# mLSTM and mixture of experts on one core: heads paired in another way, and the third expert's weights loaded at seven set places

## The chip, the cores and the metric

The kernel runs on 1 core of one Trainium2 chip. The metric is the device time in microseconds (us), the median of several executions. A core has TensorE (PE in the profile; its weight loads are PEld), VectorE (DVE), ScalarE (ACT), GpSimd (POOL) and SyncE (SP), which here issues most of the DMAs.

## The reference

First an mLSTM over 4 batches, 8 heads, 768 time steps and a head width of 40; then a mixture of 8 experts, to which each of the 3072 tokens goes by its largest logit.

```python
for t in range(S):
    m_new = np.maximum(f_gate[:, :, t] + m, i_gate[:, :, t])
    f_stab = np.exp(f_gate[:, :, t] + m - m_new)
    i_stab = np.exp(i_gate[:, :, t] - m_new)
    C = f_stab[:, :, None, None] * C + i_stab[:, :, None, None] * np.einsum('bhd,bhe->bhde', vt, kt)
    n = f_stab[:, :, None] * n + i_stab[:, :, None] * kt
    h_tilde = np.einsum('bhde,bhe->bhd', C, qt)
    denom = np.maximum(np.abs(np.einsum('bhd,bhd->bh', n, qt)[:, :, None]), 1.0)
    y[:, :, t] = 1.0 / (1.0 + np.exp(-o_gate[:, :, t])) * h_tilde / denom
...
expert_idx = np.argmax(xn @ en.T / tau, axis=1)
for e in range(E):
    h = np.maximum(x[mask] @ w1[e], 0.0)
    out[mask] = gate_w[mask, None] * (h @ w2[e])
```

## The kernel before

**The mLSTM part** runs in 24 steps `n`; a step takes 128 time steps of one batch, as two chunks `c` of 64, with all 8 heads as four pairs `a` of two heads `r`. The order of every engine's work is the order in which the code is written. A step on TensorE is, in this order: `stage_add(n, 0)` adds the first chunk's keys times values to the state sums in PSUM (two products with `j40`, line 667, carry the old state `c_st` over; line 677 adds); `stage_scores(n + 1)` makes the next step's scores (line 640); every second step transposes (`px`) and logits (`pm`); `stage_y(n)` multiplies the weighed scores `w_s` by `uv` (line 715) and the queries `q_s` by the state (line 725; `c_st` for the first chunk, `c_mid` for the second); `stage_add(n, 1)` adds the second chunk to the sums (line 677 again; not in the last four steps). ACT copies the sums to `c_mid`, DVE to `c_st`; `uv` is made by POOL (line 626), which also multiplies by the output gate (line 762) and, in six of the steps 11 to 19, makes a piece of the first expert's weights (line 208).

Of a pair, one head lies in partitions 0 to 39 and the other in 64 to 103 of `q_s` and of the state; `uv` and the state are block diagonal, 2 x 41 columns wide, the second head's block to the right. In `stage_add` each pair is two products of 41 columns with the same weights, one to the upper and one to the lower half of the output's partitions. All these matmuls are fp32, and one product stands in the trace as two matmuls and two weight loads.

**The expert part.** The first two experts run early, on their first half of tokens and then on the second. The latter loop, in the program `mm1(exps[e]["ws"], xp, ...)` with 2 x 8 feature blocks `f`, makes the tiles `hh_b` (ACT, line 396) and `hl_b` (DVE, line 398) from `ph` (TensorE, line 394, 8 matmuls each, three buffers). Between the blocks, `do(3 - e)` takes small steps from the list `todo`: the order of the remaining experts (`order`), their token lists, the gather of the third expert's tokens (`tokens`, four indirect DMAs on POOL), then the 7 loads of the third expert's weights. Load 0 and 1 are 512 KB each, load 2 is 256 KB twice (to both halves), loads 3 to 6 are 320 KB each. SP first reads six expert numbers into registers (line 1572), then issues the loads. The buffers `raw` (7) are free by then. The pieces are cast by ACT (line 205) and completed by DVE (line 208) in the loop behind, `mm2` of `po_b`. Later experts' loads are issued as their buffers come free.

Of the kernel before, what the change touches and what calls it, by code (L numbers as in the profile page):

```python
# [22 lines left out]
B, H, S, D = 4, 8, 768, 40  # L23
# [3 lines left out]
P = 128  # L27
L = 64
NW = S // P
NP = H // 2  # L30
NS = NW * B
NC = S // L
FC = F // P
# [3 lines left out]
D1 = D + 1  # L37
# [11 lines left out]

W1_AT = (11, 13, 14, 16, 17, 19)  # L50
W_AT = (10, 12, 13, 15, 16, 18, 19, 20, 22, 22, 22, 23, 23)
XW = 3 * P
PAD = NT
MID = NT // 2
# [11 lines left out]
def tile_mlstm_moe(  # L66
# [22 lines left out]
    V, G, A, T, SY = nc.vector, nc.gpsimd, nc.scalar, nc.tensor, nc.sync  # L89
# [72 lines left out]
    def load_expert(e, at=None):  # L162
        raws, ws = {}, {}
        w1_, w2_ = (w[e] if at is None else w[ds(at, 1)].rearrange("o p f -> (o p) f") for w in (w1, w2))

        def load(i):
            def go():
                raw = raws[i] = wp.tile([P, F], F32, name=f"raw_{e}_{i}", tag="raw", bufs=7)
                if i < 2:
                    SY.dma_start(raw, w1_[i * P : (i + 1) * P])  # L170
                elif i == 2:
                    SY.dma_start(raw[0:L], w1_[2 * P : DM])
                    SY.dma_start(raw[L:P], w1_[2 * P : DM])
                else:
                    c = slice(2 * (i - 3), 2 * (i - 3) + 2)
                    SY.dma_start(
                        raw[:, 0 : 2 * DM].rearrange("p (c d) -> p c d", c=2),
                        w2_.rearrange("(c p) d -> p c d", p=P)[:, c],
                    )

            return go

        def load_half(i, half):
            def go():
                c = slice(half * 512, half * 512 + 512)
                if half == 0:
                    raws[i] = wp.tile([P, F], F32, name=f"raw_{e}_{i}", tag="raw", bufs=7)
                if i < 2:
                    SY.dma_start(raws[i][:, c], w1_[i * P : (i + 1) * P, c])
                else:  # L190
                    for r0 in (0, L):
                        SY.dma_start(raws[i][r0 : r0 + L, c], w1_[2 * P : DM, c])

            return go

        def piece(i, half, eng=None, on_act=True):
            def go():
                if i < 3:
                    c = slice(half * 512, half * 512 + 512)
                    h, lo, src = ws["w1h"][:, i, c], ws["w1l"][:, i, c], raws[i][:, c]  # L200
                else:
                    c = 2 * (i - 3) + half
                    h, lo, src = ws["w2h"][:, c], ws["w2l"][:, c], raws[i][:, half * DM : (half + 1) * DM]
                if on_act:
                    A.copy(h, src)  # L205
                else:
                    V.tensor_copy(h, src)
                (eng or V).tensor_tensor(lo, src, h.bitcast(F32), ALU.subtract)  # L208

            return go  # L210

        def tiles(pool, k):
            for t in "hl":
                shape = [P, 3, F] if k == 1 else [P, FC, DM]
                ws[f"w{k}{t}"] = pool.tile(shape, F32R, name=f"w{k}{t}_{e}", tag=f"w{k}{t}")

        return dict(ws=ws, tiles=tiles, load=load, load_half=load_half, piece=piece)


# [322 lines left out]
    with ExitStack() as actx:  # L542
# [22 lines left out]
        NH, NG, NB = B * H, NJ * B * H, 3  # L565
# [11 lines left out]
        k_e, k_o, q_s, kv_s, kr_s, vr_s, uv, w_s = [], [], [], [], [], [], [], []  # L577
# [55 lines left out]
        def stage_scores(n):  # L633
            q, k = divmod(n, 2)
            s = st.setdefault(n, {})["s"] = pS.tile([P, 2, NP, L], F32, name=f"s_{n}", tag="ps")
            for c in range(2):
                for a in range(NP):
                    for r, kk in ((0, k_e), (1, k_o)):
                        cs = slice(c * L, c * L + L)
                        T.matmul(  # L640
                            s[r * L : r * L + L, c, a],
                            kk[q % NB][:, k, a, cs],
                            q_s[q % NB][:, k, a, cs],
                            start=True,
                            stop=True,
                        )
# [12 lines left out]
        def stage_add(n, c):  # L659

            q, k = divmod(n, 2)
            if c == 0:
                st[n]["y"] = pY.tile([P, 512], F32, name=f"y_{n}", tag="py")
            pc = pcv(n)
            if c == 0 and n >= B:
                for r in range(2):
                    T.matmul(  # L667
                        pc[r * L : r * L + D],
                        j40,
                        c_st[n % B][:, :, r * D1 : (r + 1) * D1],  # L670
                        start=True,
                        stop=False,
                        skip_group_check=True,
                    )
            for a in range(NP):
                for r in range(2):
                    T.matmul(  # L677
                        pc[r * L : r * L + D, a],
                        kr_s[q % NB][:, k, c, a],
                        uv[n % NB][:, c, a, r],  # L680
                        start=n < B and c == 0 and a == 0,
                        stop=True,
                        skip_group_check=True,
                    )

        def state_rows(n, dst):
            for r in range(2):
# [20 lines left out]
        def stage_y(n):  # L708

            q, k = divmod(n, 2)  # L710
            y = st[n]["y"]
            for a in range(NP):
                ya = [y[c * L : c * L + L, a * 2 * D1 : (a + 1) * 2 * D1] for c in range(2)]
                for c in range(2):
                    T.matmul(  # L715
                        ya[c],
                        w_s[n % NB][:, c, a],
                        uv[n % NB][:, c, a].rearrange("p r d -> p (r d)"),
                        start=False,
                        stop=n < B and c == 0,  # L720
                        skip_group_check=True,
                    )
                for c, state in ((0, c_st[n % B]), (1, c_mid[n % 2])):
                    if n >= B or c:
                        T.matmul(  # L725
                            ya[c],
                            q_s[q % NB][:, k, a, c * L : c * L + L],
                            state[:, a],
                            start=False,
                            stop=True,  # L730
                            skip_group_check=True,
                        )
# [393 lines left out]
        def halves(t, n, r):  # L1126
            return t.rearrange("p (g r a) -> p g r a", r=2, a=NP)[:, :, r]
# [7 lines left out]
        for c in range(2):  # L1135
            for r in range(2):
# [4 lines left out]
                    start=True,  # L1141
                    stop=True,
                )
        for r in range(2):
            r0 = r * L
# [23 lines left out]
        gr = ap1.tile([NG, NK, NG], F32, name="gr")  # L1169
# [45 lines left out]
        def gates_turn():  # L1215
            n = NJ * B
            w = n * NP
            pt = pM.tile([P, 512], F32, name="pg1", tag="pm")
            for k in range(NK):
                for c in range(2):  # L1220
                    for r in range(2):
                        at_ = (k * 2 + c) * w
# [10 lines left out]
            for k in range(NK):  # L1233
                for r in range(2):
                    at_ = 8 * w + k * w
                    T.matmul(
                        pt[r * L : r * L + L, at_ : at_ + w].rearrange("p (g a) -> p g a", a=NP),
                        onef[0:NG, 0:L],
                        halves(gr[:, k], NG, r),
                        start=True,  # L1240
                        stop=True,
                    )
# [204 lines left out]
        def do(k):  # L1447
            for _ in range(k):
                if todo:
                    todo.pop(0)()  # L1450
# [118 lines left out]
    def where():  # L1569

        at.extend(
            nc.values_load(order[0:1, j : j + 1], engines=[ET.SP], min_val=0, max_val=E - 1) for j in range(NO)
        )
        exps[2] = load_expert(2, at[0])
        todo[:] += [exps[2]["load"](i) for i in range(7)]

    def tokens():
        nonlocal xs
# [5 lines left out]
    for e in range(NE):  # L1584
        for f in range(FC):
            mm1(exps[e]["ws"], xp, slice(e * HALF, (e + 1) * HALF), f, hs, slice(e * HALF, (e + 1) * HALF))
            do(3 - e)
            if f % 4 == 1:
                first_out(2 * e + f // 4, *first_outs[2 * e + f // 4])
        if e == 0:  # L1590
            exps[2]["tiles"](wp, 1)
            todo += beyond
# [202 lines left out]
def _layout(q, k, v, i_gate, f_gate, o_gate, moe_expert_emb, moe_tau, moe_w1, moe_w2):  # L1795
# [6 lines left out]

    def dims_first(a):

        a = a.reshape(B, NP, 2, NW, P, D).transpose(3, 0, 2, 5, 1, 4).reshape(NS // 2, 2, 2, D, NP, P)
        return c(a.transpose(0, 2, 3, 1, 4, 5))

    def both_heads(a):
# [50 lines left out]
```

## Time and profile before

| | |
|---|---|
| device time, median of 3 | 339.04 us (338.65 to 343.72) |
| the profiled execution | 340.7 us, its span 338.9 us |
| TensorE busy | 313.4 us, 92% of the span |
| VectorE busy | 219.3 us, 65% |
| ScalarE busy | 162.4 us, 48% |
| GpSimd busy | 146.1 us, 43% |
| TensorE's mean granted clock | 0.978 |
| HBM read and written | 172 GB/s over the span |

The span runs from the first to the last instruction; the profiled execution has 1.8 us around it. Of TensorE, busy time counts the whole modelled duration of each matmul, and consecutive ones overlap, so how dense it is shows better in the starts of its instructions than in this share. The mLSTM part ends at about 118 us, the early experts' part at about 193 us, and six experts follow.

### The profile page before, as it was taken

The page shows a single profiled execution, that of the slowest core. Times are in us where ns is not written, and L with a number is a line of the kernel's source. Part 1 is how long each engine was busy: PE and PEld are TensorE (multiplying, and loading weights), DVE is VectorE, ACT ScalarE, POOL GpSimd, SP SyncE. Part 2 cuts the span into 40 slices and gives each one's busy share as a digit, 9 for nine tenths or more (in the row PEclk, how much of TensorE's full clock was granted, in tenths as well). Part 3 has the DMA queues.
Part 4 walks back from the last instruction along what each step waited for, and adds up shares of the span by engine and source line. Part 5 has one row for each costly group of instructions (what it writes and reads, how often), then busy time and mean ns, then how long its engine had stood idle before and what let it go on. Part 6 is the DMA issues. An engine that isn't in the chain of part 4 may idle for free.

```text
span 338.9 us, 10523 instructions
## 1 busy us (share of the span) xinstructions
PE 313.4 (92%) x4120; PEld 296.4 (87%) x4121; DVE 219.3 (65%) x626; ACT 162.4 (48%) x429; POOL 146.1 (43%) x182
## 2 busy tenths in 40 slices
PE   8897989998988888999979999999999999999991
PEld 4786979887977778999969989999999999999991
DVE  6674677896885449996645595566566585685520
ACT  4655555566655484343325465254454463463410
POOL 6657757668787169040631711240250241322121
PEclk9997999999999799999979999999999999999997
DMA  7998687997998605020392887346447458431001
GB/s 228 289 307 258 200 267 240 288 296 250 309 319 240 236 21 155 2 77 3 112 306 94 232 238 222 118 125 190 122 127 224 126 151 223 119 91 39 12 10 45
DMA packets 29344, 58.57 MB, mean 173 GB/s; under 512 B 3851, under 2 KB 18392, under 8 KB 29286
## 3 DMA queue, kind: packets, MB, share of 16 engines
q1 hardware_dynamic: 26406, 48.91, 47.3%
q0 software_dynamic: 2624, 8.48, 8.4%
q8 instruction: 34, 0.56, 0.7%
q10 hardware_dynamic: 256, 0.43, 0.4%
q14 instruction: 24, 0.20, 0.2%
HBM read 49.98 MB, written 8.19 MB: 172 GB/s over the span
## 4 chain that ended last, share of the span: by engine, by line
PE 80%; issue 5%; DVE 4%; ACT 3%; DMA 3%; POOL 2%; another core or an unknown queue 1%; POOLq 0%; SPq 0%; DVEq 0%; ACTq 0%
PE ph L394 27%; PE po L432 17%; PE s L640 5%; PE y L715 4%; PE po_b L432 4%; PE po_a L432 3%; PE y L677 3%; PE y L725 3%; PE po L419 3%; PE pt L357 2%; PE warm L1078 2%; DMA kv_s<-in_rows 2%; PE px L792 2%; PE pm L812 1%; PE y L667 1%
## 5 line engine op out<-in xcount | busy, mean ns | idle before, releaser
L451 POOL DMA_INDIRECT out<-ob,ids x20 | 20.3, 1014 | 99.6 <-DVE ob L448 73.8
L626 POOL TENSOR_TENSOR uv<-kv_s,u_t 64x328 f32<-64x328 f32 x47 | 35.5, 754 | 17.5 <-PE y L677 11.2
L432 PE MATMUL po<-w2h,hh 128*128 128x320 f32 x128 | 40.3, 315 | 0.0
L432 PE MATMUL po<-w2l,hh 128*128 128x320 f32 x128 | 39.6, 309 | 0.0
L432 PE MATMUL po<-w2h,hl 128*128 128x320 f32 x128 | 39.6, 309 | 0.0
L396 ACT ACTIVATE hh<-ph 128x448 fp32r<-128x448 f32 (+2 forms) x48 | 23.6, 491 | 33.1 <-PE ph L394 31.4
L398 DVE SCALAR_TENSOR_TENSOR hl<-ph,hh 128x384 fp32r<-128x384 f32 (+1 forms) x48 | 24.5, 511 | 14.6 <-ACT hh L396 11.1
L715 PE MATMUL y<-uv,w_s 128*64 128x82 f32 x384 | 30.3, 246 | 3.2 <-issue 2.1
L640 PE MATMUL s<-q_s,k_o 128*64 128x64 f32 x384 | 28.2, 224 | 5.2 <-issue 5.1
L394 PE MATMUL ph<-xh,w1h 128*128 128x448 f32 (+2 forms) x96 | 32.2, 338 | 0.0
L394 PE MATMUL ph<-xh,w1l 128*128 128x448 f32 (+2 forms) x96 | 32.1, 337 | 0.0
L640 PEld LDWEIGHTS s<-q_s,k_o 128*64 128x64 f32 x384 | 24.9, 138 | 6.1 <-issue 6.1
L640 PE MATMUL s<-q_s,k_e 128*64 128x64 f32 x384 | 28.3, 224 | 1.0 <-DVE w_s L649 0.7
L725 PE MATMUL y<-c_mid,q_s 128*64 128x82 f32 x192 | 28.9, 240 | 0.0
L205 ACT CAST w1h<-raw 128x512 fp32r<-128x512 f32 x48 | 28.8, 616 | 0.0
L448 DVE TENSOR_SCALAR ob<-po,gts 128x320 f32<-128x320 f32 x16 | 8.8, 551 | 28.1 <-PE po L432 28.1
L715 PEld LDWEIGHTS y<-uv,w_s 128*64 128x64 f32 x384 | 21.9, 141 | 5.5 <-issue 3.6
L208 DVE TENSOR_TENSOR w2l<-raw,w2h 128x320 fp32r<-128x320 f32 x58 | 26.5, 494 | 0.2
L640 PEld LDWEIGHTS s<-q_s,k_e 128*64 128x64 f32 x384 | 24.8, 138 | 2.1 <-DVE w_s L649 0.8
L649 DVE TENSOR_TENSOR w_s<-s,late 128x512 f32<-128x512 f32 x24 | 16.5, 686 | 14.3 <-PE s L640 9.6
L205 ACT CAST w2h<-raw 128x320 fp32r<-128x320 f32 x62 | 25.2, 461 | 0.0
L693 ACT COPY c_mid<-y 40x164 f32<-40x164 f32 x48 | 14.0, 292 | 22.1 <-PE y L677 15.4
(327 smaller groups left out, 984.4 us busy)
## 6 DMA issues: line engine op xcount, KB each, us to landing
raw<-in_w SPq DMA_DIRECT2D x32, 320.0 KB
kv_s<-in_rows SPq DMA_DIRECT2D x23, 324.0 KB
raw<-in_w SPq DMA_DIRECT2D x14, 512.0 KB
q_s<-in_qt SPq DMA_DIRECT2D x11, 512.0 KB
raw<-in_w SPq DMA_DIRECT2D x18, 256.0 KB
sig<-in_og SPq DMA_DIRECT2D x24, 160.0 KB
x_d<-x SPq DMA_DIRECT2D x24, 160.0 KB
k_e<-in_kt SPq DMA_DIRECT2D x11, 160.0 KB
```

The source lines that it names most:

```text
L205: A.copy(h, src)
L208: (eng or V).tensor_tensor(lo, src, h.bitcast(F32), ALU.subtract)
L394: T.matmul(ph, lt, rh, start=i == 0, stop=i == len(ops) - 1)
L396: A.activation(hh, ph, AF.Relu)
L398: V.scalar_tensor_tensor(hl[:, 0:full], ph[:, 0:full], 0.0, hh[:, 0:full].bitcast(F32), ALU.max, ALU.subtract)
L432: T.matmul(po[0 : ts_.stop - ts_.start, 0:DM], lt[f][:, ts_], rh[:, f], start=k == 0, stop=k == len(ops) - 1)
L451: store = G.indirect_dma_start(out=out, out_offset=bass.IndirectOffsetOnAxis(ap=slots, axis=0), in_=ob, in_offset=None, bounds_check=NT - ...
L626: (eng[r] if eng else G).tensor_tensor(uv[n % NB][rows, :, :, r], vr_s[q % NB][rows, k], u_t[rows, j, b].unsqueeze(3).broadcast_to([L, 2, ...
L640: T.matmul(s[r * L : r * L + L, c, a], kk[q % NB][:, k, a, cs], q_s[q % NB][:, k, a, cs], start=True, stop=True,)
L649: V.tensor_tensor(w_s[n % NB].rearrange("p c a t -> p (c a) t"), st[n]["s"].rearrange("p c a t -> p (c a) t"), late.unsqueeze(1).broadcast ...
L715: T.matmul(ya[c], w_s[n % NB][:, c, a], uv[n % NB][:, c, a].rearrange("p r d -> p (r d)"), start=False, stop=n < B and c == 0, skip_group_ ...
L725: T.matmul(ya[c], q_s[q % NB][:, k, a, c * L : c * L + L], state[:, a], start=False, stop=True, skip_group_check=True,)
```

## The change

**First part.** The two heads of a pair `a` now stand side by side in the columns of the state sums, in the upper half of the partitions for even `a` and in the lower half for odd `a`. So `stage_add` makes one product of 82 columns for each pair (4 in place of 8 of 41 columns), and the state's column block `m` holds one head of each of two pairs. The keys, the queries and the decay factors are laid out accordingly by the host and by one set of matmuls at the start; `stage_scores` takes other blocks in the same number; in `stage_y` all eight products of line 715 come first, then those of line 725, which now write two runs of 41 columns.

**Second part.** The third expert's loads leave the list. Load `i` is issued after feature block `W2_AT[i]` of the 16, and VectorE writes one element of its buffer first, on which the DMA waits.

```diff
+W2_AT = (4, 6, 8, 10, 11, 13, 14)
...
-        def load(i):
+        def load(i, after=None):
             def go():
                 raw = raws[i] = wp.tile([P, F], F32, name=f"raw_{e}_{i}", tag="raw", bufs=7)
+                if after:
+                    after.memset(raw[0:1, 0:1], 0.0)
...
                 for a in range(NP):
-                    for r, kk in ((0, k_e), (1, k_o)):
-                        cs = slice(c * L, c * L + L)
+                    for r in range(2):
+                        m = a // 2 * 2 + r
                         T.matmul(
                             s[r * L : r * L + L, c, a],
-                            kk[q % NB][:, k, a, cs],
-                            q_s[q % NB][:, k, a, cs],
+                            (k_e, k_o)[a % 2][q % NB][:, k, m, cs],
+                            q_s[q % NB][:, k, m, cs],
...
             for a in range(NP):
-                for r in range(2):
-                    T.matmul(
-                        pc[r * L : r * L + D, a],
-                        kr_s[q % NB][:, k, c, a],
-                        uv[n % NB][:, c, a, r],
-                        start=n < B and c == 0 and a == 0,
+                r0, m = a % 2 * L, a // 2 * 2
+                T.matmul(
+                    pc[r0 : r0 + D, m : m + 2],
+                    kr_s[q % NB][:, k, c, a],
+                    uv[n % NB][:, c, a],
+                    start=n < B and c == 0 and a < 2,
...
+            for m in range(NP):
                 for c, state in ((0, c_st[n % B]), (1, c_mid[n % 2])):
                     if n >= B or c:
                         T.matmul(
-                            ya[c],
-                            q_s[q % NB][:, k, a, c * L : c * L + L],
-                            state[:, a],
+                            yp[c * L : c * L + L, m // 2, :, m % 2],
+                            q_s[q % NB][:, k, m, c * L : c * L + L],
+                            state[:, m].rearrange("p (q d) -> p q d", q=2),
...
         exps[2] = load_expert(2, at[0])
-        todo[:] += [exps[2]["load"](i) for i in range(7)]
...
             do(3 - e)
+            if e * FC + f in W2_AT:
+                exps[2]["load"](W2_AT.index(e * FC + f), V)()
```

On TensorE, from the end of `stage_y` of step 7 to the first scores of step 9, the rows before are these (a row is a product, with its line, output, inputs and columns; the number behind a name is a buffer's):

```order
L715 MATMUL y_928<-uv_154,w_s_155 64x82 x2
L725 MATMUL y_928<-c_st_165,q_s_146 64x82
L725 MATMUL y_928<-c_mid_167,q_s_146 64x82
L677 MATMUL y_928<-uv_154,kv_s_147 40x41 x8
L812 MATMUL pm_731<-ent_138,xt_986 64x16 x10
L667 MATMUL y_1033<-c_st_162,j_169 40x164 x2
L677 MATMUL y_1033<-uv_160,kv_s_153 40x41 x8
L640 MATMUL s_1046<-q_s_152,k_e_150 64x64
L640 MATMUL s_1046<-q_s_152,k_o_151 64x64
```

and now, with line numbers moved by 4 or 5:

```order
L730 MATMUL y_872<-c_st_165,q_s_146 64x2x41
L730 MATMUL y_872<-c_mid_167,q_s_146 64x2x41
L681 MATMUL y_872<-uv_154,kv_s_147 40x82 x4
L817 MATMUL pm_691<-ent_138,xt_926 64x16 x10
L671 MATMUL y_969<-c_st_162,j_169 40x164 x2
L681 MATMUL y_969<-uv_160,kv_s_153 40x82 x4
L644 MATMUL s_978<-q_s_152,k_e_150 64x64 x2
L644 MATMUL s_978<-q_s_152,k_o_151 64x64 x2
```

The sums of a chunk are 4 products of 82 columns where 8 of 41 stood; the pair of state products is now preceded by others of its kind, not by scores' products; nothing else has moved.

On VectorE, in the second half tokens' loop from the fifth to the tenth feature block, the rows before are these:

```order
L398 SCALAR_TENSOR_TENSOR hl_b_3133<-ph,hh_b_3132 128x256
L280 TENSOR_TENSOR arrange<-arrange,gtf 128x144
L287 TENSOR_REDUCE gts<-arrange 128x24
L398 SCALAR_TENSOR_TENSOR hl_b_3135<-ph,hh_b_3134 128x256
L450 TENSOR_SCALAR ob_a_2859<-ob_a_2859,gtf 128x320
L398 SCALAR_TENSOR_TENSOR hl_b_3137<-ph,hh_b_3136 128x256
L398 SCALAR_TENSOR_TENSOR hl_b_3139<-ph,hh_b_3138 128x256
L398 SCALAR_TENSOR_TENSOR hl_b_3125<-ph,hh_b_3124 128x256
L291 TENSOR_TENSOR arrange<-arrange,caps 128x36
L293 TENSOR_REDUCE cap<-arrange 128x6
L398 SCALAR_TENSOR_TENSOR hl_b_3127<-ph,hh_b_3126 128x256
```

and now:

```order
L401 SCALAR_TENSOR_TENSOR hl_b_2957<-ph,hh_b_2956 128x256
L283 TENSOR_TENSOR arrange<-arrange,gtf 128x144
L290 TENSOR_REDUCE gts<-arrange 128x24
L171 MEMSET raw_0_3108 1x1
L401 SCALAR_TENSOR_TENSOR hl_b_2959<-ph,hh_b_2958 128x256
L453 TENSOR_SCALAR ob_a_2683<-ob_a_2683,gtf 128x320
L401 SCALAR_TENSOR_TENSOR hl_b_2961<-ph,hh_b_2960 128x256
L171 MEMSET raw_1_3137 1x1
L401 SCALAR_TENSOR_TENSOR hl_b_2963<-ph,hh_b_2962 128x256
L401 SCALAR_TENSOR_TENSOR hl_b_2949<-ph,hh_b_2948 128x256
L294 TENSOR_TENSOR arrange<-arrange,caps 128x36
L296 TENSOR_REDUCE cap<-arrange 128x6
```

Seven one-element writes have come in, one behind the block of each load; the third, for load 2, stands behind the last row. The orders of SP, POOL and ACT are unchanged.

## Rows read from the trace of the kernel before

**Rows 1.** Busy time by stage: us, each engine's busy time (instructions), PEclk, DMA share, GB/s.

```profile
8.00:28.00 20.00, 16.06 (x432) 14.32 (x429) 13.68 (x52) 12.03 (x37) 12.95 (x21) 1.00 0.89 283
28.00:104.00 76.00, 71.08 (x1993) 66.56 (x1995) 58.26 (x200) 43.03 (x132) 54.74 (x77) 0.98 0.85 274
158.00:178.00 20.00, 17.28 (x130) 16.84 (x130) 11.23 (x43) 5.57 (x16) 8.07 (x8) 0.91 0.60 180
```

**Rows 2.** The chain of work in one step: start us, us, engine, tile, line, count.

```profile
61.87 0.14 PE y L715 x4
...
62.16 0.31 PE y L677 x16
```

**Rows 3.** Two state products of one step in order of time, TensorE: start us, us.

```profile
39.92 0.23 PE L725 MATMUL y<-c_st,q_s 128*64 128x82 f32 x1
39.93 0.23 PE L725 MATMUL y<-c_mid,q_s 128*64 128x82 f32 x1
```

**Rows 4.** TensorE's waits, 8 to 104 us: us in total, times, longest.

```profile
PE s L640 <- issue: 4.3, 4, 2.5
PE y L677 <- issue: 1.3, 2, 0.7
...
PE y L715 <- issue: 0.9, 1, 0.9
```

**Rows 5.** TensorE in order of time inside one step's scores.

```profile
47.69 0.28 PE L640 MATMUL s<-q_s,k_e 128*64 128x64 f32 x2
48.88 0.22 PE L640 MATMUL s<-q_s,k_o 128*64 128x64 f32 x1 [0.91 <-issue]
```

**Rows 6.** Busy time as in Rows 1, between three such gaps of TensorE.

```profile
43.15:48.50 5.35, 4.74 (x127) 4.32 (x127) 4.21 (x16) 3.08 (x10) 3.42 (x6) 1.00 0.94 310
48.50:66.40 17.90, 17.07 (x509) 16.26 (x508) 13.88 (x49) 8.77 (x28) 11.79 (x16) 1.00 0.80 255
```

**Rows 7.** The page's DMA queues: packets, MB, share.

```profile
q8 instruction: 34, 0.56, 0.7%
```

**Rows 8.** The chain of work, 78 to 83 us.

```profile
79.33 0.71 POOL uv L626
...
80.93 0.87 POOL x L762
...
82.83 0.36 PE y L715 x4
```

**Rows 9.** Instructions on the tile raw, of GpSimd: ns min/median/max, first and last start.

```profile
L208 POOL TENSOR_TENSOR w1l<-raw,w1h x12: 1267/1281/1299, 63.3 to 128.0; 128x512 fp32r<-128x512 f32 x12
```

**Rows 10.** The chain of work, 153 to 200 us.

```profile
157.91 9.68 PE ph L394 x80
...
167.62 0.39 ACT hh_b L396
168.00 3.33 another core or an unknown queue
...
172.25 5.68 PE ph L394 x32
```

**Rows 11.** SP's DMA issues in order of time, 160 to 174 us.

```profile
166.19 1.36 SPq L170 DMA_DIRECT2D raw<-in_w  x2
167.64 0.49 SPq L172 DMA_DIRECT2D raw<-in_w  x1
...
169.85 2.61 SPq L176 DMA_DIRECT2D raw<-in_w  x4
```

**Rows 12.** Busy time as in Rows 1, around the halt of Rows 10.

```profile
170.00:172.00 2.00, 0.00 (x0) 0.00 (x0) 0.23 (x1) 0.64 (x3) 0.30 (x1) 1.00 1.03 350
...
174.00:176.00 2.00, 2.00 (x11) 2.00 (x11) 0.81 (x4) 0.38 (x1) 0.20 (x1) 0.50 1.03 252
```

**Rows 13.** A small VectorE instruction in the same loop.

```profile
173.17 0.14 DVE L300 TENSOR_REDUCE arrange<-cnt_s 128x1 f32<-128x2 f32 x1
```

**Rows 14.** ACT's first casts of the third expert's second layer, in order of time.

```profile
186.31 1.54 ACT L205 CAST w2h<-raw 128x320 fp32r<-128x320 f32 x4
```

More of the change, by code (lines that the diff above doesn't have):

```diff
@@ L636, in stage_scores @@
             for c in range(2):
+                cs = slice(c * L, c * L + L)
                 for a in range(NP):
-                    for r, kk in ((0, k_e), (1, k_o)):
-                        cs = slice(c * L, c * L + L)
+                    for r in range(2):
+                        m = a // 2 * 2 + r
                         T.matmul(
                             s[r * L : r * L + L, c, a],
-                            kk[q % NB][:, k, a, cs],
-                            q_s[q % NB][:, k, a, cs],
+                            (k_e, k_o)[a % 2][q % NB][:, k, m, cs],
+                            q_s[q % NB][:, k, m, cs],
                             start=True,
@@ L675, in stage_add @@
             for a in range(NP):
-                for r in range(2):
-                    T.matmul(
-                        pc[r * L : r * L + D, a],
-                        kr_s[q % NB][:, k, c, a],
-                        uv[n % NB][:, c, a, r],
-                        start=n < B and c == 0 and a == 0,
-                        stop=True,
-                        skip_group_check=True,
-                    )
+                r0, m = a % 2 * L, a // 2 * 2
[4 more added lines that the diff above has]
+                    start=n < B and c == 0 and a < 2,
+                    stop=True,
+                    skip_group_check=True,
+                )
         def state_rows(n, dst):
@@ L711, in stage_y @@
             y = st[n]["y"]
+            yp = y[:, 0 : H * D1].rearrange("p (a q r d) -> p a q r d", a=NP // 2, q=2, r=2)
             for a in range(NP):
-                ya = [y[c * L : c * L + L, a * 2 * D1 : (a + 1) * 2 * D1] for c in range(2)]
                 for c in range(2):
                     T.matmul(
-                        ya[c],
+                        y[c * L : c * L + L, a * 2 * D1 : (a + 1) * 2 * D1],
                         w_s[n % NB][:, c, a],
@@ L725, in stage_y @@
                         T.matmul(
-                            ya[c],
-                            q_s[q % NB][:, k, a, c * L : c * L + L],
-                            state[:, a],
+                            yp[c * L : c * L + L, m // 2, :, m % 2],
+                            q_s[q % NB][:, k, m, c * L : c * L + L],
+                            state[:, m].rearrange("p (q d) -> p q d", q=2),
                             start=False,
@@ L1236, in gates_turn @@
                     T.matmul(
-                        pt[r * L : r * L + L, at_ : at_ + w].rearrange("p (g a) -> p g a", a=NP),
+                        pt[r * L : r * L + L, at_ : at_ + w].rearrange("p (g a r) -> p g a r", a=NP // 2, r=2),
                         onef[0:NG, 0:L],
-                        halves(gr[:, k], NG, r),
+                        gr[:, k].rearrange("p (g r a q) -> p g a r q", r=2, a=NP // 2, q=2)[:, :, :, :, r],
                         start=True,
@@ L1803, in dims_first @@
     def dims_first(a):
-        a = a.reshape(B, NP, 2, NW, P, D).transpose(3, 0, 2, 5, 1, 4).reshape(NS // 2, 2, 2, D, NP, P)
+        a = a.reshape(B, 2, 2, 2, NW, P, D).transpose(4, 0, 2, 6, 1, 3, 5).reshape(NS // 2, 2, 2, D, NP, P)
         return c(a.transpose(0, 2, 3, 1, 4, 5))
```

## The prediction

> **What bounds the kernel now.** I read the busy time by stage first, then the chain of waits, then single stretches in order of time. From 28 to 104 us, most of the mLSTM, TensorE is busy for 71.1 of 76 us and VectorE for 58.3 [rows 1]: TensorE sets the pace there, and the chain of a step is a row of its products, end to end [rows 2]. What TensorE idles in the mLSTM it mostly does not idle for another engine: from 8 to 104 us the waits put down to "issue", time in which it waited for nothing the profile shows, are 4.3 + 1.3 + 0.9 = 6.5 us in seven gaps [rows 4]. They stand in the middle of a group of equal products: the scores of one step stop at 47.7 and go on at 48.9 [rows 5], with no semaphore between. Between one such gap and the next lie 254 matmuls and weight loads, and between that and a third 1017 [rows 6], 4 times 254. One DMA queue carries instructions in 34 packets of 0.56 MB together, 16 KB each [rows 7]; TensorE's 4120 matmuls and 4121 loads divided by 34 are 242 a packet. So I take the gaps for a block of some 256 instructions that comes late, while the data's DMAs keep the engines 85% busy [rows 1]; some blocks in between come in time.
>
> In the second half tokens' loop, 158 to 178 us, the chain is TensorE's 80 matmuls, then a halt: 3.33 us in which ACT waited for something that the profile does not name, then the granted clock at 0.50, its lower level of 1.2 GHz [rows 10, 12]. After that TensorE is dense to the end.
>
> **The change, part by part.** I sum against the profiled execution, 340.7 us (span 338.9 and 1.8 around it), and take the difference over to the median, 339.04, which is 1.7 lower.
>
> *Columns of the sums.* A chunk's 8 products of 41 columns are 16 matmuls and take 0.31 us [rows 2], two at a time, one for each half of the output. The 4 products of 82 columns are 8 matmuls, 4 pairs. Products of that width are in the same trace: line 715's 4 matmuls (2 pairs) take 0.14 us [rows 2], so 4 pairs take 0.28. That they go in pairs with different weights and different columns is seen in line 725, where c_st and c_mid start 0.01 us apart [rows 3]; the new order alternates the halves in the same way. There are 704/16 = 44 chunks: 44 x 0.03 = 1.3 us. In the six steps where POOL also makes a weight piece, it is POOL that ends last: two `uv` parts, the gate and a piece are 0.71 + 0.74 + 0.87 + 1.28 = 3.6 us [rows 8, 9], and the chain from 79 to 83 us runs through it. What TensorE saves there is idle time: 1.1 us remain.
>
> The Trainium skill ("TensorE: Matmul & The Clock Gate", Back-to-back issue gap) gives products of 1 to 64 columns one cost, a floor of about 25 ns. Were that so here, the page's estimate would be 704 x 25 ns less 352 x 36.7 ns, a gain of 4.7 us, and the sum 3.6 us lower. The trace's 16 matmuls in 0.31 us are 19 ns each, under that floor, so it is not what binds in these pairs, and I give it no chance.
>
> *Instructions.* 352 matmuls and as many weight loads go. From 8 to 104 us that is 672 of the 4849 that run there [rows 1], 14%. A block lasts 256/56 = 4.6 us of work now (3988 instructions in 71 us) and 5.3 us then, so a late block has 0.7 us more before it is missed. Taken off each of the seven gaps, as far as it goes, that is 0.7 from the three longest and the whole of the shorter four (6.5 - 2.5 - 0.9 - 0.9 = 2.2): some 4.3 us. Bounds: 0 if the cuts fall on worse places, as all block ends move; 6.5 if all gaps close. I take 2.8, between 4.3 and the middle of the bounds' lower half: new ends meet the same queue of data, and from 79 us on POOL is close behind.
>
> *Order in `stage_y`, other layouts.* The same products in the same number; line 725 now reads `c_mid` later than before, which can only help its one wait. The writes in two runs of 41 columns are not in the trace; line 640's and line 725's fixed pace says that a pair is bound by its columns, so nothing, and 0.01 us a pair (44 x 4 pairs, 1.8 us) at worst. At the start two small sets of matmuls only read other places.
>
> *The loads.* Seven one-element writes on VectorE are 0.14 us each [rows 13], at most 1.0 us if all were on the path; three buffers of `ph` cover them: 0. What would the later issue change? SP is busy with its registers until 166.19, when load 0 goes out anyway; load 1 follows at once, as its write stands behind a block that is done by then. Load 2 went out from 167.64 and will wait for the ninth block; loads 3 to 6 went out from 169.85 [rows 11]. The halt has begun by 168.00 [rows 10], before any of these four, and in it the DMA engines carry what was issued ahead (1.03 busy, 350 GB/s [rows 12]), loads 0 and 1 and the gather, which remain where they are. So I expect the halt to remain: 0. The later landing is covered: the second layer's casts begin at 186.31 [rows 14], and the last of the blocks that release loads ends by 178. If the cover were gone, ACT would wait some 1 us for 320 KB at 350 GB/s. Bounds: a loss of 1 us, a gain of 4.5, below.
>
> Sum: 1.1 + 2.8 + 0 + 0 = 3.9 us; 340.7 - 3.9 = 336.8, and **335.1 us** of the median. A measurement of this kernel tells about 2%, 6.8 us, from no change, so this is within.
>
> **The rivals.**
>
> *The halt goes too.* At the pace of the first 80 matmuls, 9.68 us, the loop's 128 take 15.5 us from 157.91 and end at 173.4; they end at 177.93 [rows 10]. If loads 2 to 6 in one row are what blocks, spacing them gives the whole 4.5 us, half clock included: 335.1 - 4.5 = 330.6. For it: later experts, whose loads go out singly as buffers come free, show no such halt. Against it: the times of issue above. Chance 0.2.
>
> *The instruction blocks give nothing.* The seven gaps stay or move, or POOL and the data's DMAs take the pace in the mLSTM (DMA 85% busy on average [rows 1], and it has the same bytes to move in less time). Then only the columns are left: 339.04 - 1.1 = 337.9. The Trainium skill ("Runtime: NRT & Kernel Launch", Instruction fetch mechanics) has the blocks of 256 instructions, and says that crossing into the next is mostly hidden; by that this is the case. The trace has seven idle gaps whole blocks apart, which speaks against hidden. Chance 0.21.
>
> *The products no longer pair (slower).* If the products of 82 columns with different weights went one after the other, 8 matmuls would take 8 x 0.07 = 0.56 us in place of 0.31: 0.25 x 44 = 11 us, and 339.04 - 2.8 + 11 = 347.2 us. It makes the kernel slower than before once a quarter of the pairs fail (2.8 us), by 2% once nearly all do. Against it: lines 715 and 725. Chance 0.03.
>
> **How the numbers follow.** My forecast has 0.56, the rivals 0.2, 0.21 and 0.03. The forecast's own range is 331.4 (all gaps closed) to 338.5. The range to hold 8 in 10 takes in most of both larger rivals: 329.5 to 339.2. Faster by over 2% means below 332.3: most of the first rival, and a little of the forecast, 0.21. Slower by over 2%: the third, 0.03, and 0.01 for what I don't see. Within: 0.75.
>
> **What would show it.** The sums' group should have 352 matmuls, and a chunk take 0.28 us in the chain; TensorE's "issue" waits from 8 us to the end of the mLSTM should fall from 6.5 to 3 or 4 us, still whole blocks apart; the mLSTM should end some 4 us earlier; the halt at ACT should stand in the half tokens' loop as before, some 4 us earlier in the run. If the loop takes 15.5 us, the loads were its cause and I am wrong there. If the gaps are as long as before, the blocks were not bound by the time between them. If a chunk takes over 0.5 us, the pairing is gone.

## The result, and the profile of the changed kernel

The changed kernel takes **335.99 us**, median of 20 runs (333.67 to 340.45), beside 341.91 us for the kernel before in the same set (20 runs, 337.02 to 345.21). The ratio is 0.9895, with a 95% interval of 0.9864 to 0.9925: faster by 1%, and within the 2% that the chances speak of. Executions over 1.5% above the fastest of their kernel are left out of this and every other ratio, so it is not the ratio of the two medians. Taken to the 339.04 us of the first runs, it is 335.5 us. The profiled execution has a span of 334.1 us, 338.9 before.

Busy time by stage, the changed kernel (us, then busy time and instructions of TensorE, its weight loads, VectorE, ScalarE, GpSimd; granted clock, DMA share, GB/s), to hold against [rows 1]:

```profile
8.00:28.00 20.00, 18.42 (x419) 16.18 (x418) 14.61 (x54) 13.46 (x41) 13.86 (x23) 1.00 0.92 292
28.00:104.00 76.00, 69.34 (x1760) 64.81 (x1755) 58.54 (x205) 43.56 (x135) 55.37 (x76) 0.98 0.87 277
158.00:178.00 20.00, 17.35 (x126) 16.94 (x125) 9.50 (x40) 6.64 (x17) 8.10 (x8) 0.91 0.68 209
```

From 8 to 104 us TensorE issues 2179 matmuls where it issued 2425, and is farther on in the program at the end of them. What it waits for there (us in total, times, longest), beside [rows 4]:

```profile
PE px L797 <- ACT xc L790: 3.0, 3, 1.8
PE y L681 <- issue: 2.1, 1, 2.1
PE pm L817 <- DVE ent L827: 1.4, 1, 1.4
PE s L644 <- DVE w_s L653: 1.0, 2, 0.5
PE y L719 <- ACT c_mid L697: 0.3, 1, 0.3
```

The seven waits for "issue", 6.5 us together, are now one of 2.1. To the end of the mLSTM, the stretch that the prediction names, they are 8.8 us before and 4.2 now; behind 104 us both kernels have six short ones. But other engines are waited for: `xc`, `ent`, `w_s` and `c_mid` make 5.7 us, where it was 2.0 before. The last state product of the mLSTM (line 730) starts at 112.6 us; before, at 116.4.

A step in the chain of waits (start, us, engine, tile, line, count), beside [rows 2]:

```profile
64.83 0.72 PE y L719 x16
65.56 0.57 PE y L730 x16
66.12 0.28 PE y L681 x8
...
70.32 2.12 issue
72.44 0.40 PE y L681 x5
```

A chunk's sums take 0.28 us as 8 matmuls; it was 0.31 as 16 [rows 2]. The `y` products take 0.72 + 0.57 = 1.29 us, as they did when the two lines alternated (from 60.87 to 62.16 us in the chain of before). The remaining halt for "issue" stands inside a row of equal products, as in [rows 5].

The half tokens' loop in the same view, beside [rows 10]:

```profile
154.21 9.71 PE ph L397 x80
...
163.94 0.39 ACT hh_b L399
164.32 3.24 another core or an unknown queue
...
168.48 5.58 PE ph L397 x32
```

The halt is still there, 3.24 us after 3.33, and the loop ends at 174.06, 19.85 us after its start; before it took 20.02. So of 4.8 us of span, 3.7 are gained ahead of this loop; 0.2 are gained in it and lost again behind it; and 1.1 come from the very end, behind GpSimd's last issue of `out`: 4.1 us to the end of the span, 5.2 before, where both kernels do the same. Counted from the start of the loop, SP issues load 2 at 11.0 us, 9.7 before, and loads 3 to 6 from 15.7 us on, 11.9 before.

### The profile page after: what moved, and what is told of

Its sections match the earlier page's. It is cut to its first block, busy times and chain, and to the rows that moved or that the text cites. A ratio compares the mean times of both kernels' runs of the same rounds, so it can differ in the third digit from the quotient of the medians.

```text
span 334.1 us, 9812 instructions
## 1 busy us (share of the span) xinstructions
PE 310.5 (93%) x3768; PEld 293.1 (88%) x3769; DVE 218.4 (65%) x633; ACT 162.6 (49%) x429; POOL 146.8 (44%) x182
## 4 chain that ended last, share of the span: by engine, by line
PE 79%; DVE 4%; issue 4%; DMA 4%; ACT 3%; POOL 3%; another core or an unknown queue 1%; SPq 1%; POOLq 0%; DVEq 0%; ACTq 0%
PE ph L397 27%; PE po L435 17%; PE s L644 4%; PE po_b L435 4%; PE y L719 4%; PE po_a L435 4%; PE y L730 3%; PE y L681 3%; PE po L422 3%; PE pt L360 2%; DMA sig<-in_og 2%; PE warm L1083 2%; PE px L797 2%; DMA raw<-in_w 2%; PE pm L817 2%
## 5 line engine op out<-in xcount | busy, mean ns | idle before, releaser
L644 PE MATMUL s<-q_s,k_e 128*64 128x64 f32 x384 | 24.3, 223 | 1.2 <-DVE w_s L653 1.0
L397 PE MATMUL ph<-xl,w1h 128*128 128x448 f32 (+2 forms) x96 | 24.6, 337 | 0.0
L322 POOL DMA_INDIRECT xs<-x_d,ids x20 | 21.4, 1071 | 6.9 <-issue 5.5
L211 DVE TENSOR_TENSOR w1l<-raw,w1h 128x512 fp32r<-128x512 f32 x36 | 24.4, 688 | 0.0
L644 PE MATMUL s<-q_s,k_o 128*64 128x64 f32 x384 | 24.2, 222 | 0.0
L435 PEld LDWEIGHTS po<-w2l,hh 128*128 128x128 f32 x128 | 24.1, 188 | 0.0
L435 PEld LDWEIGHTS po<-w2h,hh 128*128 128x128 f32 x128 | 24.1, 188 | 0.0
L435 PEld LDWEIGHTS po<-w2h,hl 128*128 128x128 f32 x128 | 24.0, 188 | 0.0
```

The lines of the kernel that those rows point to most:

```text
L322: G.indirect_dma_start(out=xs[0 : c.shape[0], a, 0:DM], out_offset=None, in_=x_d[0:rows], in_offset=bass.IndirectOffsetOnAxis(ap=c, axis=0 ...
L397: T.matmul(ph, lt, rh, start=i == 0, stop=i == len(ops) - 1)
L435: T.matmul(po[0 : ts_.stop - ts_.start, 0:DM], lt[f][:, ts_], rh[:, f], start=k == 0, stop=k == len(ops) - 1)
L644: T.matmul(s[r * L : r * L + L, c, a], (k_e, k_o)[a % 2][q % NB][:, k, m, cs], q_s[q % NB][:, k, m, cs], start=True, stop=True,)
```

## The experiments

All ratios are to the kernel before, measured beside it in the same set of runs; sets on different chips have different times (the kernel before: 332.5, 330.5 and 340.9 us in the three timed sets), so only ratios are compared across them.

**The two parts, one at a time.** First part alone: the loads go back to the list.

```diff
+        todo[:] += [exps[2]["load"](i) for i in range(7)]
...
-            if e * FC + f in W2_AT:
-                exps[2]["load"](W2_AT.index(e * FC + f), V)()
```

> The first part of the change alone; the third expert's seven loads are issued from the list, as before the change. Theory (all of the gain is in the mLSTM part, the loads are worth nothing): a ratio of 0.988 to 0.993 to the kernel before, the mLSTM shorter by 3 to 4 us, the halt of 3.3 us in the half tokens' loop unchanged. Rival (the spaced loads give a part that the profile of one execution doesn't show): over 0.994.

Second part alone: the reverse edit on the kernel before.

> The second part of the change alone, on the pairing of before. Theory: a ratio of 0.998 to 1.002, the halt of about 3.3 us in the half tokens' loop as before. Rival (the loads matter by themselves): 0.996 or less, and the loop of 128 matmuls takes under 19 us.

Measured: 0.9866 [0.9801, 0.9931] with the pairing alone and 0.9988 [0.9943, 1.0034] with the loads alone. All that can be measured comes from the pairing. In both profiles the half tokens' loop has no halt; the chain of waits of the first one, and under it that of the second:

```profile
151.91 15.21 PE ph L397 x128
```

```profile
157.39 15.21 PE ph L397 x128
```

That was expected of neither. With the loads in one row as before, the 128 matmuls run through in 15.21 us on this chip; with the loads spread, they halt for 3.24 us on the chip of the first profiles. The profiles of all the kernels that can be read to their end agree: the halt is in the six of the first set and of the last one below, with the loads in one row (two) or spread (four), and in none of the five of the other two sets, again with either order. So the halt goes with the chip or the set, not with the loads' times. Why is not shown.

**The number of instructions.** The changed kernel, with each product of 82 columns split into two of 41:

```diff
-                T.matmul(
-                    pc[r0 : r0 + D, m : m + 2],
-                    kr_s[q % NB][:, k, c, a],
-                    uv[n % NB][:, c, a],
+                for r in range(2):
+                    T.matmul(
+                        pc[r0 : r0 + D, m + r],
+                        kr_s[q % NB][:, k, c, a],
+                        uv[n % NB][:, c, a, r],
...
```

> The changed kernel with each sums' product of 82 columns split into two of 41 columns with the same weights, so that TensorE has as many instructions as before the change (704 matmuls in the group), while the pairing of heads, the order in the y step and the loads stay changed. Theory (the gain is in the number of TensorE's instructions: blocks of them come late): waits of TensorE put down to issue between 8 and 104 us are back at 5 to 10 us, and the ratio to the kernel before is 0.996 to 1.004. Rival (the gain is in the order of the products and the layout, not in the count): issue waits of 0 to 2 us, and a ratio of 0.985 to 0.993.

Measured: 1.0007 [0.9962, 1.0052], the whole gain gone, with the new layout, the new order in `stage_y` and the new loads all in place. TensorE's waits from 8 to 104 us:

```profile
PE y L731 <- issue: 2.9, 2, 1.9
PE s L644 <- issue: 2.8, 3, 2.3
PE y L682 <- issue: 1.5, 2, 1.3
```

That is 7.2 us, in seven waits; in the kernel with the loads alone it is 9.5 us in eight. With the pairing alone it is one wait:

```profile
PE s L644 <- issue: 0.2, 1, 0.2
```

The count of TensorE's instructions makes the difference; the columns' own 1.3 us is too small to be seen beside an interval of 0.9%.

**What the waits for issue are.** The trace holds each packet of the instruction queue. In the changed kernel TensorE enters a block of 256 at 65.61 us (counted in its row). The transfers from then on, by queue (packets, MB, share), first from 65.7 to 69.8 us, then from 69.8 to 71.0:

```profile
DMA packets 663, 1.19 MB, mean 291 GB/s; under 512 B 96, under 2 KB 344, under 8 KB 663
## 3 DMA queue, kind: packets, MB, share of 16 engines
q1 hardware_dynamic: 663, 1.19, 93.6%
```

```profile
q1 hardware_dynamic: 112, 0.27, 85.0%
q8 instruction: 1, 0.02, 6.0%
```

For 4.1 us the data's queue holds 94% of the DMA engines and no instructions come; the one packet of 16 KB starts at 69.83 and is in at 70.98. TensorE in order of time:

```profile
70.01 0.30 PE L681 MATMUL y<-uv,kv_s 128*40 128x82 f32 x3
72.44 0.41 PE L681 MATMUL y<-uv,kv_s 128*40 128x82 f32 x5 [2.12 <-issue]
```

It stops after the third of eight matmuls, with the last instruction of its block, and goes on 1.46 us after the packet is in. So it is at every late block. From 8 to 104 us the fourteen traces have 50 gaps of over 0.4 us between two starts of TensorE at this one place in every 256 of its instructions, and each of them ends 1.1 to 1.7 us after the end of a packet, median 1.45. There is one packet for each block entered there, as if the next one were asked for then; it starts up to 4.4 us later (mean 2.1 us in the kernel before, and in the changed one), takes 1 us, and 1.45 us later it can be used. In the kernel before a block lasts 4.6 us on average without the halt at its end, so by these means a packet that starts over some 2 us late is missed; in the changed kernel, with fewer, longer instructions and other waits between them, a block lasts 5.7 us, and only starts later than some 3 us are.

The Trainium skill ("Runtime: NRT & Kernel Launch", Instruction fetch mechanics) has the sequencer fetch the next 16 KiB block of 256 instructions while it executes the current one, and calls the cost of crossing into it mostly hidden. The trace agrees on the block and on one packet per crossing. It disagrees on hidden: 5.0 to 9.8 us of TensorE's 96 are put down to it in the six traces with the old count, 0 to 2.1 in the eight with the new one.

**Is it the data's transfers that make the packet late?** The kernel before with the output gate's rows loaded for the first four steps alone:

```diff
-                sigs[j] = tp.tile([P, B, DM], F32, name=f"sig_{j}", tag="sig", bufs=2)
-            SY.dma_start(sigs[j][:, b], og[:, n])
+                sigs[j] = sigs[0] if j else tp.tile([P, B, DM], F32, name=f"sig_{j}", tag="sig", bufs=2)
+            if j == 0:
+                SY.dma_start(sigs[j][:, b], og[:, n])
```

> The kernel before with the output gate's rows loaded for the first four steps alone and used for all others (the output gate of the later steps is left out): 20 loads of 160 KB less, 3.2 MB of some 26 MB in the mLSTM. If instruction blocks are late because the data's transfers keep the DMA engines full, TensorE's issue waits between 8 and 104 us fall to under 4 us (6.5 and 9.5 in the two profiles with this number of instructions) and the ratio is 0.98 to 0.99. Rival (blocks are late whatever the data's transfers): issue waits of 5 to 10 us, a ratio of 0.996 to 1.003.

And that with the first experts' weights moved to the steps from 20 on as well:

```diff
-W_AT = (10, 12, 13, 15, 16, 18, 19, 20, 22, 22, 22, 23, 23)
+W_AT = (20, 20, 20, 21, 21, 21, 22, 22, 22, 22, 22, 23, 23)
...
-            if n in W1_AT:
-                exps[0]["piece"](*PIECES1[W1_AT.index(n)], G)()
+            if n in (22, 23):
+                for p in PIECES1[3 * n - 66 : 3 * n - 63]:
+                    exps[0]["piece"](*p, G)()
```

> The kernel before, with the output gate's rows of steps 4 to 23 not loaded (that gate is left out) and with the first two experts' weights loaded from step 20 on, their first pieces made in steps 22 and 23: between 50 and 92 us only keys, values, queries and the stores of x are moved. Only that stretch is read, the total time says nothing. If an instruction block comes late because its packet stands behind the data's packets, TensorE's issue waits from 50 to 92 us fall to under 0.6 us, from 1.3, 2.3, 2.6, 2.8 and 2.8 us in the five profiles with this number of instructions. Rival (blocks are late whatever the data's transfers): 1.3 us or more, at a DMA share of 0.5 to 0.65 in place of 0.79 to 0.90.

With that gate left out the tokens fall on the experts otherwise, and the run takes some 6200 us; only the mLSTM's stretch is read. The first gave 9.8 us of issue waits at a DMA share of 0.77, where under 4 were expected. The second, 50 to 92 us:

```profile
50.00:92.00 42.00, 39.76 (x1149) 37.14 (x1148) 30.38 (x112) 21.80 (x70) 26.36 (x33) 1.00 0.72 226
```

```profile
PE pm L813 <- issue: 0.7, 1, 0.7
PE y L678 <- issue: 0.6, 1, 0.6
PE s L641 <- issue: 0.6, 1, 0.6
PE y L716 <- issue: 0.2, 1, 0.2
```

2.1 us, inside the 1.3 to 2.8 of the other profiles, and the packets start as late as ever (2.0 us on average). The theory's numbers failed twice. It isn't refuted: the DMA share fell to 0.72 only, since the same keys and values are still loaded, and where the DMA engines are idle, from 118.8 to 120.8 us, the packet in the changed kernel starts 0.54 us after the crossing at 120.87. Mean shares of 0.72 to 0.90 over this stretch show no difference. The share right behind a crossing does: over the 252 blocks entered from 8 to 104 us in the fourteen traces, the packet starts 1.1 us later on average, and never over 1.8, where the data's transfers fill under 0.6 of the DMA engines in the next 2 us (27 blocks), and 2.6 us later, up to 4.2, where they fill them wholly (66 blocks). That speaks for a burst in front of the packet, as the rows of 65.7 to 71.0 do; no run has tried it alone, so the reason for the lateness stays open.

**Do the products pair because they alternate between the halves?** The changed kernel with the sums' products in another order:

```diff
-            for a in range(NP):
+            for a in (0, 2, 1, 3):
                 r0, m = a % 2 * L, a // 2 * 2
```

> The changed kernel with the sums' products in the order 0, 2, 1, 3, so that two products of 82 columns into the same half of the output follow each other. If products overlap only when the next one in the row goes to the other half, a chunk takes 0.45 to 0.56 us in place of 0.28, 7 to 12 us in all, a ratio of 1.01 to 1.025 to the kernel before. If the halves take their products each from its own queue, however far apart they stand in the row, a chunk stays at 0.28 to 0.35 us and the time is that of the changed kernel, a ratio of 0.987 to 0.995.

Measured: 0.9862 [0.9787, 0.9937], the time of the changed kernel. TensorE in order of time:

```profile
65.60 0.48 PE L681 MATMUL y<-uv,kv_s 128*40 128x82 f32 x8
65.88 0.74 PE L817 MATMUL pm<-ent,xt 128*64 128x16 f32 x20
66.43 0.49 PE L671 MATMUL y<-c_st,j 128*40 128x164 f32 x4
66.73 0.48 PE L681 MATMUL y<-uv,kv_s 128*40 128x82 f32 x8
67.01 0.32 PE L644 MATMUL s<-q_s,k_e 128*64 128x64 f32 x4
```

The group behind a chunk starts 0.28 us after it, as in the changed kernel. So the two halves of the output need not alternate product by product; four matmuls to one half and then four to the other overlap as well.

**What ends last now?** Three things were tried. First, the output gate's rows loaded a step earlier, since ACT waited 11.6 us for them from 8 to 104 us in the changed kernel:

```diff
-            for m in {0: (), 1: (0, 1), 2: (2, 3)}.get(n, (n + 1,)):
+            for m in {0: (), 1: (0, 1), 2: (2, 3), 3: (4, 5)}.get(n, (n + 2,)):
```

> The changed kernel with the output gate's rows (sig) loaded one step earlier, the same bytes. Theory (what now ends last in the mLSTM's dense part is the landing of sig, which ACT and GpSimd wait for, and through xc TensorE's transposes): TensorE's waits for xc between 8 and 104 us fall from 3.0 to under 1 us, and the time by 1 to 3 us against the changed kernel, a ratio of 0.981 to 0.988. Rival (the DMA engines are full, and another transfer is late in its place): waits of the same sum for another tile, a ratio of 0.987 to 0.993.

Second, these loads left out from the changed kernel, with the edit shown above:

> The changed kernel with the same loads left out (the output gate of steps 4 to 23). Theory (after the change it is the data's transfers that end last, through ACT and GpSimd, in the dense part): TensorE's waits for xc, c_mid, k_o and ent between 8 and 104 us fall from 5 to 7 us to 2 or 3, and the ratio to the kernel before is 0.965 to 0.98. Rival (GpSimd's and ACT's own work ends last): the waits stay, and the ratio is that of the changed kernel, 0.985 to 0.992.

The first gave 0.9863 [0.9792, 0.9935], no better than the pairing alone in the same set (0.9866). In both, ACT's waits for the rows are gone from its list, and TensorE's waits stand: with the rows a step earlier 2.2 us for `xc` and 2.1 for `c_mid`, without them 2.4 and 2.4. What ACT waits for longest in the second, from 40 to 104 us:

```profile
ACT xc L791 <- POOL x L768: 15.2, 10, 2.6
```

So these transfers were not what ended last; GpSimd stands in their place. For the second this rests on the waits alone, as its whole run takes some 6200 us. Third, GpSimd's row with the changed kernel once more, at a step with a weight piece, and ACT's:

```profile
83.58 0.86 POOL L767 TENSOR_TENSOR x<-x,sig 128x320 f32<-128x320 f32 x1
85.53 1.29 POOL L211 TENSOR_TENSOR w1l<-raw,w1h 128x512 fp32r<-128x512 f32 x1 [1.09 <-ACT w1h L208]
86.78 1.55 POOL L629 TENSOR_TENSOR uv<-kv_s,u_t 64x328 f32<-64x328 f32 x2
```

```profile
84.48 0.46 ACT L790 COPY xc<-x 128x320 f32<-128x320 f32 x1 [0.45 <-POOL x L767]
84.84 0.61 ACT L208 CAST w1h<-raw 128x512 fp32r<-128x512 f32 x1
```

GpSimd gates `x`, ACT copies it and then casts the piece's upper part, GpSimd waits 1.09 us for that cast, and `uv` for the step after next stands behind. The edit makes each piece one step later than its cast (`part=1` makes the cast alone, `part=2` GpSimd's piece alone); the second kernel gives the pieces to VectorE; the third puts the first edit into the kernel before; the fourth is the changed kernel again.

```diff
             if n in W1_AT:
-                exps[0]["piece"](*PIECES1[W1_AT.index(n)], G)()
+                exps[0]["piece"](*PIECES1[W1_AT.index(n)], part=1)()
...
+            if n - 1 in W1_AT:
+                exps[0]["piece"](*PIECES1[W1_AT.index(n - 1)], G, part=2)()
...
```

> The changed kernel with GpSimd's six weight pieces (w1l) made one step later than ACT's casts that they read, in the same place of the step. Theory (what now ends last in the mLSTM's second half is a round trip between GpSimd and ACT: the gated x, ACT's copy xc, ACT's cast, GpSimd's piece, then uv): GpSimd's waits for w1h fall from 8 to 10 us to under 2, TensorE's waits for xc and c_mid between 8 and 104 us from 3 to 5.5 us to under 2.5, and the time by 1 to 3 us, a ratio of 0.978 to 0.986 to the kernel before. Rival (GpSimd's work, not its waiting, is what ends last, or the data's transfers): the same waits by another name, and the ratio of the changed kernel, 0.986 to 0.991.

```diff
-                exps[0]["piece"](*PIECES1[W1_AT.index(n)], G)()
+                exps[0]["piece"](*PIECES1[W1_AT.index(n)], V)()
```

> The changed kernel with the same six pieces made by VectorE, each behind ACT's cast as before. If GpSimd's work itself ends last, this takes 7.7 us from it and the time falls by 1 to 3 us, a ratio of 0.978 to 0.986; VectorE, busy for some 60 of 76 us there, would now wait for ACT's cast in its own row, and if that matters as much, the ratio is 0.987 or more, with waits of TensorE for VectorE's w_s or c_st in place of those for xc.

> The kernel before with its six pieces a step later, as in the kernel with the changed pairing. Theory (before the change TensorE's late instruction blocks and its columns set the pace, and the round trip was hidden): a ratio of 0.996 to 1.002, TensorE's issue waits of 6 to 10 us between 8 and 104 us unchanged. Rival (the round trip cost as much before): 0.99 to 0.995.

> The changed kernel once more, beside the others on this chip. Theory: a ratio of 0.985 to 0.993 to the kernel before; TensorE's issue waits between 8 and 104 us under 2.5 us; and the halt of 3 us in the half tokens' loop is absent if it was absent in the kernel with the first part alone (it would then belong to the chip or the execution, not to the loads), present if the loads' times make it.

Measured, in one set: pieces a step later **0.9755** [0.9699, 0.9811]; pieces on VectorE 0.9782 [0.9721, 0.9844]; the kernel before with pieces a step later 0.997 [0.9905, 1.0034]; the changed kernel again 0.9912 [0.9875, 0.9949]. From 8 to 104 us the changed kernel again has this among GpSimd's waits:

```profile
POOL w1l L211 <- ACT w1h L208: 7.1, 5, 2.5
```

With the pieces a step later, GpSimd waits for no cast any more:

```profile
83.84 0.86 POOL L766 TENSOR_TENSOR x<-x,sig 128x320 f32<-128x320 f32 x1
84.66 1.27 POOL L210 TENSOR_TENSOR w1l<-raw,w1h 128x512 fp32r<-128x512 f32 x1
85.89 1.02 POOL L561 TENSOR_TENSOR ss_all<-ss_all,half 128x4 f32<-128x4 f32 x1
```

TensorE's waits for `xc` and `c_mid` from 8 to 104 us fall from 4.9 us to 1.4; first the changed kernel again, then the one with the pieces a step later:

```profile
PE y L719 <- ACT c_mid L697: 2.5, 4, 1.0
PE px L797 <- ACT xc L790: 2.4, 5, 0.9
```

```profile
PE px L796 <- ACT xc L789: 1.4, 2, 1.0
```

These two profiles don't account for the whole gain: other waits grow as these fall (three late blocks of over 0.4 us among them, where the changed kernel again has none), the last state product starts at 108.2 us in place of 110.2, and the spans are 1.5 us apart, where the two ratios differ by 1.6%, some 5 us. The profiled execution of the changed kernel took 332.7 us, its median is 336.85; where the 4 us between them go is not shown.

In the changed kernel again the half tokens' loop takes 19.84 us with its loads spread (TensorE idles for 2.42 us in it), so spreading doesn't free it there either. The kernel before with the pieces a step later has its loads in one row, and its chain has the halt too:

```profile
169.05 3.39 another core or an unknown queue
```

With 331.47 us for the pieces a step later, beside 336.85 for the changed kernel and 340.91 for the one before, that kernel beats both. That the same edit does nothing that can be measured in the kernel before, where TensorE lacks its instructions, shows that the round trip came to cost time through the change; the interval there leaves room for up to 0.95%. Which part of the round trip counts, GpSimd's waiting or its work, is not told apart: taking the work away altogether gave about the same.

## Why the prediction was right, point by point

The forecast was 335.1 us; 335.5 on the same scale, and the ratio's interval (334.4 to 336.5) holds it. Two of its terms were off, in opposite directions. (The upper end of its own range, 338.5, is not worked out; with no gap closed its terms give 337.9.)

*Columns, 1.1 of 1.3 us.* A chunk takes 0.28 us in 8 matmuls, as worked out from line 715. The reason given for the pairing, that the products alternate between the halves, is not needed: the order 0, 2, 1, 3 is as fast. The rival in which products no longer pair (347.2 us, slower) did not come about.

*Instructions, 2.8 us.* The cause was right: waits for blocks that come late, gone with the count and back with it. The size was not: of 6.5 us, 3 to 4 were to remain; 2.1 remained in one profile of the changed kernel and 0.2 in the other, so 4.4 to 6.3 us went, at or above the estimate of 4.3. It was cut to 2.8 because new ends "meet the same queue of data" and POOL is close behind; the packet's delay did stay the same (2.1 us on average before and after), but the block became longer by more than the 0.7 us put down, 5.7 us in place of 4.6, since the new waits lie in it too.

*"From 79 us on POOL is close behind"*, priced at 0.2 us of the columns and named as a reason for 2.8. This was the second miss: waits for ACT and VectorE grew by 3.7 us in the first profile and ate most of what the instructions gave. The longest, 1.8 us for `xc` up to 64.07 us, stood behind the landing of the gate's rows, on which ACT waited until 62.74; one of 0.9 us that ended at 99.98 stood behind GpSimd's `x`.

*The sum* came out in part by luck. Counted from start to start of TensorE's matmuls, from the first product of the sums to the last state product, the mLSTM went from 108.1 to 104.6 us in the first two profiles: late blocks cost 5.7 us less (1 in place of 7), waits for other engines 4.6 us more, and the rest of the row takes 2.5 us less, where 1.3 us were put down to columns. Where the other 1.2 us come from is not shown. So the rival in which GpSimd and the data's DMAs take the pace was nearer than the forecast on what the instructions are worth after the new waits: it put that at nothing, the forecast at 2.8 us, and it is 1.1 us here. It named the right engine. Of the data's transfers, the gate's rows could come a step earlier for no gain that can be measured; what gave a gain was GpSimd's round trip with ACT.

*Order in `stage_y`, 0.* 1.29 us before and after. *The loads, 0.* 0.9988 by themselves. The forecast that the halt would remain was right, and the reason given, that the transfers in it remain, was not tested: the halt is absent on another chip with either order of the loads. Without it the loop takes 15.21 us; the rival's 15.5 was close to the right price for a thing that the loads don't decide.

*The end of the run*, 1.1 us of the 4.8 by which the span is shorter, was in no term; both kernels do the same there, so one profile each doesn't make it an effect of the change.

## What to carry to other kernels

Where a dense engine stops in the middle of equal instructions with nothing to wait for, count its instructions from one such stop to the next, and look when the instruction queue's packets land: fewer, wider instructions can then be worth several times their own time. When such a limit goes, look for the next one in the same steps before the edit is priced: here GpSimd's pieces, which waited for ACT while ACT waited for GpSimd, cost nothing that could be measured before the change, and 1.6% behind it. An edit that measures as nothing may be worth trying again once another has gone in.

## What was not expected of the hardware

- After every late block TensorE goes on 1.1 to 1.7 us (median 1.45, 50 gaps in fourteen traces) after its packet has landed; the packet itself takes 1 us for 16 KB.
- Matmuls to the two halves of the output's partitions overlap though four to one half are issued ahead of four to the other: 0.28 us for 8 of 82 columns in either order.
- The halt in the half tokens' loop, 3.24 to 3.39 us where the chain names it, appears in the profiles of some sets and not of others, whichever way the loads are issued. With it the loop takes some 20 us (19.85 in the changed kernel), without it 15.21; behind it the granted clock is at its lower level, 1.2 GHz (0.50 from 170 to 172 us in the changed kernel).
- A late block can cost clock too. In the changed kernel the granted clock is 0.50, 1.2 GHz, from 74 to 77 us, behind the halt of 2.12 us at 70.32. In the fourteen traces eleven late blocks set two starts of TensorE over 2 us apart; five of them are followed by such a stretch, six are not. Busy time by stage, as in the section on the result:

```profile
72.00:74.00 2.00, 1.56 (x38) 1.45 (x39) 0.15 (x2) 1.21 (x3) 0.81 (x1) 0.89 0.91 288
74.00:77.00 3.00, 3.00 (x34) 2.67 (x34) 1.14 (x3) 1.57 (x5) 2.88 (x4) 0.50 0.83 291
77.00:79.00 2.00, 2.00 (x56) 1.81 (x54) 0.81 (x6) 0.46 (x1) 1.89 (x3) 1.00 0.18 60
```
